# Words of the weights merged by GpSimd from the fourth item on, and the second unit's attention steps placed anew, in a one-core Trainium2 kernel

## Chip, cores, metric

The kernel runs on one core of one Trainium2 chip. The metric is the device time of one execution in microseconds (us), lower is better. "Clock" is the granted clock of TensorE as a share of full speed.

## The reference

A gated linear recurrence per head, then a two-layer block with ELU:

```python
f = 1.0 / (1.0 + np.exp(-f_logit))                      # q, k, v, f_logit: (4, 8, 768, 48)
for t in range(S):
    state = f[:, :, t, :, None] * state + np.einsum('bhd,bhe->bhde', k[:, :, t], v[:, :, t])
    y[:, :, t] = np.einsum('bhd,bhde->bhe', q[:, :, t], state)
x = y.transpose(0, 2, 1, 3).reshape(3072, 384)
h = x @ w_in                                            # w_in: (384, 2048)
g = np.where(h > 0, h, np.exp(np.minimum(h, 0)) - 1)
out = g @ w_out                                         # w_out: (2048, 384)
```

The two weights come as 64-bit floats. The kernel computes in 32 bits, so it must first turn every pair of 32-bit words into one fp32 word.

## The kernel before

The tokens are cut into 12 units of 256. While TensorE does the block for one unit (`up`: first product with the ELU behind it, `down`: second product), the attention of a later unit is worked in between, at numbered steps T. An even step does one `up`, an odd step one `down`. The weights come in 16 items, each used for the first time at its own step. An item goes through four hands: a transfer, a split on VectorE (two instructions), a lowering on ScalarE, and a merge:

```python
def split(n):
    ...
    bits = held[n] = sb.tile([128, 2 * DM], I32, tag="bits", name=f"bits{n}")     # two buffers
    nc.vector.tensor_scalar(out=bits[:], in0=hi, scalar1=3, scalar2=0x3FFFFFF8,
        op0=ALU.logical_shift_left, op1=ALU.bitwise_and)
    nc.vector.tensor_scalar(out=hi, in0=hi, scalar1=-(2**30), scalar2=None, op0=ALU.bitwise_and)

def lower(n):
    ...
    nc.scalar.activation(raw.bitcast(U16)[:, 2::4], raw.bitcast(U32)[:, 0::2], AF.Copy, scale=2.0**-29)

def merge(n):
    ...
    nc.vector.tensor_tensor(out=to.bitcast(I32), in0=bits, in1=hi, op=ALU.add)
    ...
    fetch(n + AHEAD)                                      # AHEAD = 7

def attention(u, first, then):
    ...
    at_step(then[1], lambda: advance(u))                          # TensorE: state increments
    at_step(then[2], *(lambda c=c: step(u, c) for c in range(NC)))   # VectorE: four additions
    at_step(then[3], lambda: kept.append(scores(u)), lambda: mask(u, kept[0]))
    at_step(then[4], lambda: outputs(u))
    at_step(then[5], lambda: carried(u))                          # ends with the small copies of xt
```

The schedule is manual: in the traces every engine works its instructions in the order in which this loop writes them.

```python
attention(1, (), A1)                        # second unit: A1 = (2, 4, 4, 5, 7, 9)
...
for T in range(NU * NFT):
    P = T // 2
    ...
    if T % 2 == 0 and P and order[P - 1][0] < DIRECT:
        elu(P - 1)
    for f in plan.pop(T, ()):               # attention, merges, loads of this step
        f()
    if T % 2 == 0:
        up(P)
    elif P >= LAG:
        down(P - LAG)
    for n in later.pop(T, ()):              # splits and lowerings two steps ahead of the merge
        split(n)
        lower(n)
```

The scores of the second unit use the two PSUM banks that the four additions read. And `up` of item 6 in the order (near 67 us) is the first that reads `xts[1]`, the second unit's rows. These are complete only when two copies of 48 KB, from one part of the tile to another, have landed:

```python
(nc.sync if u > 1 else nc.scalar).dma_start(
    out=x[GAP[r] : GAP[r] + PAD, 0:NKT], in_=x[frm : frm + D, NKT])
```

## Time and profile before

| | before |
|---|---|
| median, range of the first three runs | 569.17 us, 569.11 to 569.18 |
| span of the profiled run, clock | 567.4 us, 0.996 |
| TensorE waits in sum | 11.5 us, all before 44 us |
| first `up` product starts | 29.25 us |
| last down products start | 561.41 us |

A line of the waits view reads: waiting engine, tile and line, what ended the wait, then the sum, the number and the longest, in us. A line of a timeline reads: start, us, engine, line, operation, output<-input, and in brackets the idle time before it. The lines themselves stand in the prediction.

### The profile page before, as it was taken

Reading aid. Unit: us, or ns where it says so; the run is one execution under the profiler, and the core shown is the slowest. Engines: PE = TensorE matmul, PEld = TensorE weight load, DVE = VectorE, ACT = ScalarE, POOL = GpSimd, SP = SyncE. Lnnn points to the kernel's source line nnn. Section 1 sums busy time; section 2 is a strip of 40 time slices with the busy share of each in tenths; the row PEclk is TensorE's granted clock in tenths of the full one; section 3 lists DMA queues with packets and bytes.
Section 4 is the critical chain, followed back from the end, with each engine's and each line's share of the span. In section 5 each row is a group of like instructions: output and inputs, shape, how many; then the busy total and the mean of one; then the engine's idle time right before and its main releaser. Section 6 shows DMA issues by size and latency. Waiting matters only on the chain.

```text
span 567.4 us, 15202 instructions
## 1 busy us (share of the span) xinstructions
PE 550.2 (97%) x6226; PEld 501.8 (88%) x6226; DVE 395.2 (70%) x765; ACT 229.3 (40%) x417; POOL 266.3 (47%) x530
## 2 busy tenths in 40 slices
PE   6879999999999999999999999999999999999996
PEld 3457777778999999999999999999999999999995
DVE  8798485835976795885785885786786876745543
ACT  3297737334343443434333343343333343333331
POOL 6510027642374474465366357257257348325332
PEclk9998999999999999999999999999999999999999
DMA  8989780060025125215216216216206203201001
GB/s 207 259 215 297 174 223 14 2 161 29 2 50 140 58 60 143 73 45 152 79 36 155 85 37 154 84 38 154 84 20 172 84 9 72 85 2 36 29 2 35
DMA packets 37902, 53.27 MB, mean 94 GB/s; under 512 B 3680, under 2 KB 27648, under 8 KB 37824
## 3 DMA queue, kind: packets, MB, share of 16 engines
q1 hardware_dynamic: 37024, 51.62, 34.6%
q8 instruction: 51, 0.84, 0.6%
q10 hardware_dynamic: 800, 0.59, 0.5%
q14 instruction: 27, 0.22, 0.1%
HBM read 44.04 MB, written 4.72 MB: 86 GB/s over the span
## 4 chain that ended last, share of the span: by engine, by line
PE 92%; DVE 3%; DMA 2%; issue 1%; ACT 1%; POOL 1%; SPq 0%; DVEq 0%; ACTq 0%; POOLq 0%
PE psH L878 35%; PE psM L977 33%; PE psM L955 8%; PE psH L923 6%; PE psS L701 2%; PE psY L739 2%; PE psY L759 2%; PE psU_a L724 2%; PE psT L665 2%; DMA f<-f 1%; DVE f L627 1%; DMA f<-in_f_logit_dram 1%; ACT area L569 1%; DVE bits L559 0%; PE psY L804 0%
## 5 line engine op out<-in xcount | busy, mean ns | idle before, releaser
L878 PE MATMUL psH<-xt,wi 128*128 128x128 f32 (+1 forms) x960 | 177.1, 293 | 0.0
L942 POOL TENSOR_TENSOR sums<-gg 128x128 f32<-128x128 f32 x160 | 69.5, 455 | 210.8 <-DVE gg L932 202.5
L878 PEld LDWEIGHTS psH<-xt,wi 128*128 128x128 f32 x960 | 135.9, 192 | 0.8
L910 ACT ACTIVATE gg<-hh 128x512 f32<-128x512 f32 x80 | 50.5, 631 | 205.9 <-DVE hh L900 140.5
L878 PE MATMUL psH<-xt,area 128*128 128x128 f32 x640 | 110.5, 275 | 0.0
L878 PEld LDWEIGHTS psH<-xt,area 128*128 128x128 f32 x640 | 96.9, 192 | 4.1
L887 DVE TENSOR_TENSOR hh<-psH,u 128x256 f32<-128x256 f32 x80 | 33.8, 423 | 88.7 <-ACT u L885 88.7
L977 PE MATMUL psM<-area,sums 128*128 128x192 f32 x480 | 91.2, 326 | 0.0
L977 PEld LDWEIGHTS psM<-area,sums 128*128 128x128 f32 x480 | 80.1, 190 | 0.2 <-POOL sums L942 0.2
L977 PE MATMUL psM<-wo,gg 128*128 128x192 f32 x320 | 68.1, 335 | 0.0
L617 POOL TENSOR_TENSOR k<-k,f 128x256 f32<-128x256 f32 x48 | 39.4, 822 | 57.1 <-DMA area<-in_moe_w_in_dram 35.0
L627 DVE RECIPROCAL f<-f 128x256 f32<-128x256 f32 x36 | 62.8, 1747 | 1.3
L911 ACT ACTIVATE gg<-gg 128x512 f32<-128x512 f32 x96 | 60.6, 631 | 3.0
L932 DVE SCALAR_TENSOR_TENSOR gg<-gg,hh 128x512 f32<-128x512 f32 x80 | 55.7, 696 | 1.8 <-ACT gg L911 1.8
L977 PEld LDWEIGHTS psM<-wo,gg 128*128 128x128 f32 x320 | 50.2, 190 | 1.9
L900 DVE TENSOR_TENSOR hh<-psH,u43h 128x256 f32<-128x256 f32 (+1 forms) x160 | 49.8, 353 | 2.7
L923 PE MATMUL psH<-xt,wi 128*128 128x256 f32 x192 | 44.5, 381 | 1.4 <-DVE wi L577 1.2
L942 POOL TENSOR_TENSOR sums<-gg,sums 128x128 f32<-128x128 f32 x80 | 42.8, 535 | 6.3
L955 PE MATMUL psM<-wo,gg 128*128 128x384 f32 x128 | 45.4, 498 | 0.0
L885 ACT COPY u<-psH 128x128 f32<-128x128 f32 x80 | 21.0, 263 | 59.3 <-PE psH L878 59.3
L923 PEld LDWEIGHTS psH<-xt,wi 128*128 128x128 f32 x192 | 35.9, 190 | 8.6 <-issue 1.6
L900 DVE TENSOR_TENSOR u43h<-psH,hh 128x256 f32<-128x256 f32 x80 | 33.9, 423 | 13.4 <-PE psH L878 13.0
(97 smaller groups left out, 721.9 us busy)
## 6 DMA issues: line engine op xcount, KB each, us to landing
area<-in_moe_w_out_dram SPq DMA_DIRECT2D x8, 768.0 KB, 8.9
again<-in_moe_w_in_dram SPq DMA_DIRECT2D x16, 384.0 KB, 4.1
again<-in_moe_w_out_dram SPq DMA_DIRECT2D x16, 384.0 KB, 3.5
k<-in_k_dram SPq DMA_DIRECT2D x12, 384.0 KB, 4.8
q<-in_q_dram SPq DMA_DIRECT2D x12, 384.0 KB, 5.5
v<-in_v_dram SPq DMA_DIRECT2D x12, 384.0 KB, 5.9
area<-in_moe_w_in_dram SPq DMA_DIRECT2D x8, 576.0 KB, 7.2
out_dram<-o SPq DMA_DIRECT2D x38, 96.0 KB, 1.7
```

Of the source, the lines that this page charges most:

```text
L617: e.tensor_tensor(out=t[n][:, p], in0=t[n][:, p], in1=t["f"][:, p, "kq".index(n)], op=ALU.mult)
L627: nc.vector.reciprocal(f[:, p, 1], f[:, p, 0])
L878: nc.tensor.matmul(to, lhsT=lhs, rhs=rhs, start=(n == 0), stop=True, skip_group_check=True)
L887: add = lambda to, x, y: nc.vector.tensor_tensor(out=to, in0=x, in1=y, op=ALU.add)
L900: add = lambda to, x, y: nc.vector.tensor_tensor(out=to, in0=x, in1=y, op=ALU.add)
L910: nc.scalar.activation(g[:], h, AF.Relu, scale=-1.0)
L911: nc.scalar.activation(g[:], g[:], AF.Exp, scale=-1.0)
L923: nc.tensor.matmul(ph[:, i], lhsT=wi[j][:, kt, i * 128 : (i + 1) * 128], rhs=xts[m][:, kt, :], start=(kt == 0), stop=(kt == NKT - 1),)
L932: nc.vector.scalar_tensor_tensor(out=g[:], in0=g[:], scalar=-1.0, in1=phs.pop(P), op0=ALU.add, op1=ALU.max)
L942: nc.gpsimd.tensor_tensor(out=s[:, i], in0=x, in1=y, op=op)
L955: nc.tensor.matmul(pm[t][:], lhsT=g[:, i, t * 128 : (t + 1) * 128], rhs=wo[:, 2 * j + i, :], start=(j == 0 and i == 0), stop=(j == NP - 1 ...
L977: nc.tensor.matmul(pm[bank][:, half * DH : (half + 1) * DH], lhsT=x, rhs=y, start=first, stop=(j == NP - 1), skip_group_check=True,)
```

## The change

The intent is to take 13 of the 16 merges from VectorE, which was full near 40 us, to GpSimd, which was idle there, and to move the second unit's scores behind the first down product.

```diff
+    M0 = 3
...
-    A1 = (2, 4, 4, 5, 7, 9)
+    A1 = (2, 3, 4, 6, 7, 9)
...
-            nc.vector.tensor_tensor(out=to.bitcast(I32), in0=bits, in1=hi, op=ALU.add)
+            e = nc.gpsimd if n >= M0 else nc.vector
+            e.tensor_tensor(out=to.bitcast(I32), in0=bits, in1=hi, op=ALU.add)
```

## The prediction

> **What bounds the kernel now.** I read the page first: the busy shares and the chain that ended last.
>
> ```profile
> PE 550.2 (97%) x6226; PEld 501.8 (88%) x6226; DVE 395.2 (70%) x765; ACT 229.3 (40%) x417; POOL 266.3 (47%) x530
> ...
> PE 92%; DVE 3%; DMA 2%; issue 1%; ACT 1%; POOL 1%; SPq 0%; DVEq 0%; ACTq 0%; POOLq 0%
> ```
>
> TensorE holds 97% of the span and 92% of the chain. A change on VectorE and GpSimd can therefore win only what TensorE loses to waits, or to a lower clock. The view of TensorE's waits over the whole run lists nine, 12.3 us in sum (3.3 + 2.6 + 2.0 + 1.2 + 0.9 + 0.6 + 0.5 + 0.2 + 0.2), and the timeline shows all of them before 44 us. From there on TensorE has no gap. Which can the change touch? Items 0, 1 and 2 of the weights stay on VectorE, and item 3 is merged at 38.72 us, so all that lies before that moment stays. Two waits are left, both in front of the second unit's scores:
>
> ```profile
> PE psS L701 <- issue: 2.6, 1, 2.6
> ...
> PE psS L701 <- DVE state L682: 0.2, 1, 0.2
> ```
>
> "issue" says that the profile saw no releaser. The timeline of VectorE gives it: the scores (42.78 us) reuse the two banks that the four state additions read, and the third addition of four from 41.37 us, 0.46 us apart, ends just there. Why are the additions so late?
>
> ```profile
> 37.24 0.97 DVE L559 TENSOR_SCALAR bits<-area 128x768 int32<-128x768 int32 x1
> 38.24 0.57 DVE L563 TENSOR_SCALAR area<-area 128x768 int32<-128x768 int32 x1
> 38.72 0.95 DVE L577 CUSTOM_DVE_ANT_0 wo<-area,bits 128x1536 uint16<-128x1536 uint16 x1
> 39.70 0.56 DVE L559 TENSOR_SCALAR bits<-area 128x768 int32<-128x768 int32 x1
> 40.30 0.56 DVE L563 TENSOR_SCALAR area<-area 128x768 int32<-128x768 int32 x1
> 40.78 0.68 DVE L932 SCALAR_TENSOR_TENSOR gg<-gg,psH 128x512 f32<-128x512 f32 x1
> 41.37 1.77 DVE L682 TENSOR_TENSOR state<-psU_a,state 128x192 f32<-128x192 f32 x4
> ```
>
> VectorE works without a pause: a split (two instructions), the merge of item 3, a split, the activation's end, the additions. The merge at 38.72 is what the change takes away. The view by windows, cut into lengths of 3.41 us, shows that the gap costs twice (columns: length, then busy time of PE, PEld, DVE, ACT, POOL, then granted clock, DMA share, GB/s):
>
> ```profile
> 29.98:33.39 3.41, 2.16 (x11) 1.61 (x10) 2.94 (x4) 2.52 (x3) 0.73 (x1) 1.00 1.06 245
> ...
> 40.22:43.63 3.41, 0.64 (x23) 0.56 (x27) 3.00 (x9) 3.37 (x4) 0.00 (x0) 1.00 1.05 279
> 43.63:47.04 3.41, 3.41 (x59) 2.38 (x50) 3.34 (x6) 1.67 (x2) 0.00 (x0) 0.50 1.06 233
> ```
>
> After a window with 0.64 us of TensorE work the clock is 0.50 for 3.41 us: 1.7 us of work lost. A window with 2.16 us (gap 1.25 us) has no such sequel. So the place costs 2.6 + 0.2 + 1.7 = **4.5 us**, and that is the most the change can win. GpSimd is idle there:
>
> ```profile
> 72.77 0.72 POOL L617 TENSOR_TENSOR k<-k,f 128x256 f32<-128x256 f32 x1 [34.98 <-DMA area<-in_moe_w_in_dram]
> ```
>
> **What the Trainium skill says.** (1) "GPSIMD Engine Reference", 3.1, elementwise side by side: a two-input add of 2048 fp32 takes 4497 ns on GpSimd and 2293 ns on VectorE. The trace agrees in kind: GpSimd's product of 128x256 takes 0.72 us undisturbed. (2) The same page, 4.1, engine selection: an add whose tensors are all one 32-bit integer type is exact on GpSimd. No GpSimd integer add is in this trace; on VectorE the merge shows as a custom instruction over 1536 uint16, so the result should stay right. (3) "SBUF — State Buffer", who interferes with whom: a VectorE instruction in a two-port mode, or with two SBUF inputs, and a GpSimd instruction that reads SBUF exclude one another for a whole instruction. The trace agrees: the GpSimd product at 36.46 us, beside the merge on VectorE at 36.25, took 1.33 us in place of 0.72, and the split behind it, at 37.24, 0.97 in place of 0.56. (4) "TensorE: Matmul & The Clock Gate", part 1: an idle window of about 3.4 us brings the half clock. The windows above agree in length, but here 0.64 us of work did not prevent it.
>
> **The change part by part.** *Moved:* 13 of 16 merges (items 3 to 15). VectorE is rid of 13 x 0.97 = 12.6 us. GpSimd gets 13 new instructions. Estimate of one from the trace: 0.455 us for 128x128 and 0.72 for 128x256, so 0.265 us more per 128 columns, and 0.455 + 5 x 0.265 = 1.78 us for 768 columns; 13 x 1.8 = 23 us. Neither sum is on the path.
>
> *Added without being written:* splits and merges share two "bits" buffers. The split of item n + 2 may start only when the merge of item n is done. On one engine that was free; now VectorE waits for GpSimd, and GpSimd for ScalarE's lowering. With the port exclusion, both hold VectorE up.
>
> *Placement:* of the second unit, the scores go from step 5 to 6 and the advance from 4 to 3. The additions stay at 4. TensorE has nothing else in step 3, so the advance keeps its place in TensorE's order. But the first down product (step 5) now stands before the scores (step 6) and fills the hole, if item 3 is merged by then. In return the mask on VectorE comes later, behind the split of item 7 and the end of the third activation, and the outputs of step 7 need it.
>
> A ledger with the durations above (a split 1.1 us, an activation's end 0.6, a mask 1.2, a lowering 1.8, two together 3.7; up 2.6, down 2.7, scores or outputs 1.1):
> - Lowering of item 3 ends 37.96. Its merge gets the port after the first split instruction: 38.2 to 40.0. TensorE ends its up product at 40.0; down runs 40.1 to 42.8 and no longer waits for the scores.
> - VectorE's second split instruction of item 4 waits for the port until 40.0, ends 40.5; split of item 5 to 41.6; activation's end to 42.2; third addition ends 43.6, fourth 44.05. Scores begin 43.7, bulk 44.1 to 45.0: 1.1 us of gap.
> - Lowering of 4: 40.5 to 42.3, merge to 44.2; up follows, 45.0 to 47.6. Lowering of 5 to 44.1, merge 44.2 to 46.0.
> - Split of 6 waits for merge 4 and then for the port that merge 5 holds: 46.0 to 47.1. Split of 7 (its data landed at 46.1: issue at 37.8, 8.3 us to landing) to 48.2, activation's end to 48.8, mask to 50.0.
> - Outputs at 50.1, where before they began at 51.34: a new gap of 2.5 us, yet 1.2 to 1.3 us earlier, since the half clock (1.7 us) is gone while about 0.7 us of idle time came on top.
>
> Behind that TensorE sets the pace again. I checked the later meeting points in the old frame: item 13 is merged 88.1 to 89.9, then the last products of unit 2 are ready near 91.3, the transposes start at 92.6; the mixes run 5 us late near 103 us, but GpSimd stands idle for 1.4, 1.1 and 4.0 us between 106 and 118 us, so the blend at 118.4 keeps its time. Nothing changes after 125 us. Sum: 569.17 - 1.3 = **567.9 us**.
>
> **The rivals.**
> - *The hole is filled and no other opens.* For: the author moved the scores for just that. It would take the whole 4.5 us: 564.7. Against: the mask can't come before item 7 has landed (46.1), which gives 46.1 + 1.1 + 0.6 + 1.2 = 49.1 for the outputs, so even without any port conflict some 2.1 to 2.3 us are won: about 567.0.
> - *The new gap before the outputs brings the half clock in its turn.* It lies wholly between 47.05 and 50.46 in my ledger and leaves TensorE about 1 us of work there; the trace has 0.64 us as too little and 2.06 as enough. Then 1.7 us go again: about 569.6.
> - *VectorE becomes the bound through port and buffers.* If GpSimd takes the next merge before VectorE has got its split in, the additions slip by some 2 us, and a merge of over 2 us makes it likelier. Against: ScalarE's lowerings come 1.8 us apart, which leaves the port free in between. It would make about 571.
> - *Late merges collide with unit 2's scaling or the mixes,* and a wait appears near 90 us. My slack is 1.3 us; with merges of 2.5 us it is nearly gone. Up to 1 us.
>
> **Range and chances.** Centre 567.9; the good rival 567 or, with luck in the landing times, somewhat below; the bad ones 569.6 to 571. The range is 565.8 to 570.4. 2% is 11.4 us: more than twice what the place can give, and more than any loss I can construct from 13 instructions of 1.8 us next to a TensorE without gaps. Faster by over 2%: 0.01; within: 0.98; slower: 0.01.
>
> **What would show it right or wrong.** GpSimd integer adds of 128x768 at 1.6 to 2.1 us each, longer beside splits; splits on VectorE of up to 2 us where they wait for the port. In TensorE's waits, the 2.6 us before the scores gone or down to about 1, and a new wait before the first output products (line 739) of about 2.5 us. In the windows, no 0.50 after 43.6 us, perhaps one after 50.5. No TensorE wait between 60 us and the end. Wrong would be: a new wait near 90 us, a TensorE that runs through, merges far off 1.8 us, or a half clock that stays where it was.

## More of the kernel before

Between the start of the first up product and the start of TensorE's last two products lie 561.41 - 29.25 = **532.16 us**. I call this the stretch. It leaves out the start and the last stores; it is the better measure of what an order of instructions is worth, and the experiments are compared by it.

## The result

The changed kernel took 569.69 us in the median of four runs (568.47 to 570.13), the kernel before 569.14 (568.74 to 569.18). The ratio is 1.0008, with a 95% interval of 0.999 to 1.0026. A ratio here is the mean time of one kernel's fast runs over that of the other's of the same rounds, so not quite the ratio of the medians quoted. A second set of six runs gave 568.90 us against 569.00, ratio 0.9995 (0.9974 to 1.0015). The change moves the time by nothing that these runs can see. All outputs are right.

The page of the changed kernel, busy shares and the chain that ended last:

```profile
PE 551.5 (97%) x6226; PEld 502.4 (89%) x6226; DVE 389.3 (69%) x752; ACT 228.9 (40%) x417; POOL 289.7 (51%) x543
...
PE 91%; DMA 4%; POOL 1%; DVE 1%; issue 1%; ACT 1%; SPq 0%; ACTq 0%; DVEq 0%; POOLq 0%
```

VectorE is rid of 13 instructions, and GpSimd has 23.4 us more. But VectorE's busy time fell by 5.9 us only, not by the 12.6 of the merges. The time in which a VectorE instruction stands at the port (the access to SBUF that both engines share, point 3 of the prediction) counts as busy: the 32 split instructions took 24.8 us in place of 19.3, and the scaling of the state 4.4 in place of 3.2, which makes up the missing 6.7 us. TensorE's waits in front of the scores and of the first down product:

```profile
PE psS L703 <- issue: 1.6, 1, 1.6
...
PE psM L957 <- POOL wo L579: 0.5, 1, 0.5
```

Of 2.6 us, 1.6 are left, and 0.5 are new: the down product waits for the merge on GpSimd. VectorE's timeline, to be set beside that of before:

```profile
38.28 1.09 DVE L564 TENSOR_SCALAR area<-area 128x768 int32<-128x768 int32 x1
41.10 0.56 DVE L560 TENSOR_SCALAR bits<-area 128x768 int32<-128x768 int32 x1 [1.73 <-POOL wo L579]
41.69 2.08 DVE L564 TENSOR_SCALAR area<-area 128x768 int32<-128x768 int32 x1
43.69 0.67 DVE L934 SCALAR_TENSOR_TENSOR gg<-gg,psH 128x512 f32<-128x512 f32 x1
44.29 1.59 DVE L684 TENSOR_TENSOR state<-psU_a,state 128x192 f32<-128x192 f32 x4
```

and GpSimd's beside it:

```profile
38.20 0.73 POOL L619 TENSOR_TENSOR q<-q,f 128x256 f32<-128x256 f32 x1 [5.49 <-DMA f<-f]
38.88 2.18 POOL L579 TENSOR_TENSOR wo<-bits,area 128x768 int32<-128x768 int32 x1
41.41 1.95 POOL L579 TENSOR_TENSOR wi<-bits,area 128x768 int32<-128x768 int32 x1 [0.34 <-ACT area L570]
```

This is the heart of it. The merge of item 3 is gone from VectorE, yet the additions start at 44.29 us, where before they started at 41.37 (in a run whose first up product began 0.41 us earlier). The split of item 5 waited 1.73 us for the merge of item 3, and its second half then took 2.08 us in place of 0.56, since the merge of item 4 had come in between at 41.41. And the merge of item 3 itself was late: its lowering was through at 38.41 us, but GpSimd was then busy until 38.93 with the scaling of q, which had waited 5.49 us for a copy of 48 KB (`f<-f`, 5.7 us from issue to landing; 4.4 in the kernel before). The windows view (columns as in the prediction) shows the second half of the cost:

```profile
43.63:47.04 3.41, 1.64 (x45) 1.23 (x47) 3.20 (x7) 2.96 (x3) 1.25 (x1) 0.87 1.05 307
47.05:50.46 3.41, 3.41 (x41) 2.92 (x34) 3.34 (x6) 1.50 (x1) 0.59 (x1) 0.63 1.05 318
```

The half clock is still there, from about 46.2 to 49.6 us, some 2.6 us later than before. Before the outputs no gap is left in this run: TensorE came to them late enough. The net over this place can be read at the fifth up product (the one after the second unit's outputs and the second down product), counted from the first: 55.12 - 29.25 = 25.87 us before, 55.60 - 29.66 = 25.94 in the changed kernel, 53.94 - 28.09 = 25.85 in its second profile. The stretch is 561.69 - 29.66 = 532.03 us, 0.1 below that of before.

### The profile page after: what moved, and what is told of

The parts are those of the page before. It is cut to its first block, busy times and chain, and to the rows that moved or that the text cites. A ratio compares the mean times of both kernels' runs of the same rounds, so it can differ in the third digit from the quotient of the medians.

```text
span 567.3 us, 15209 instructions
## 1 busy us (share of the span) xinstructions
PE 551.5 (97%) x6226; PEld 502.4 (89%) x6226; DVE 389.3 (69%) x752; ACT 228.9 (40%) x417; POOL 289.7 (51%) x543
## 4 chain that ended last, share of the span: by engine, by line
PE 91%; DMA 4%; POOL 1%; DVE 1%; issue 1%; ACT 1%; SPq 0%; ACTq 0%; DVEq 0%; POOLq 0%
PE psH L880 35%; PE psM L979 33%; PE psM L957 7%; PE psH L925 6%; DMA area<-in_moe_w_in_dram 2%; PE psS L703 2%; PE psY L741 2%; PE psY L761 2%; PE psU_a L726 2%; PE psT L667 2%; DMA f<-f 1%; POOL k L619 1%; DMA f<-in_f_logit_dram 0%; POOL wo L579 0%; POOL q L619 0%
## 5 line engine op out<-in xcount | busy, mean ns | idle before, releaser
L902 DVE TENSOR_TENSOR hh<-psH,u43h 128x256 f32<-128x256 f32 (+1 forms) x160 | 49.6, 352 | 2.7
```

What stands on the lines that cost most here:

```text
L902: add = lambda to, x, y: nc.vector.tensor_tensor(out=to, in0=x, in1=y, op=ALU.add)
```

## The experiments

Each kernel was timed in five rounds beside the kernel before, on the same chip. The spread of a kernel's runs was 2 to 5 us, so the ratios have intervals of about plus or minus 0.2 to 0.3%. The stretch comes from one profile each; the two profiles of the changed kernel differ by 0.9 us, so smaller differences of the stretch say nothing. In the 14 profiles the first up product starts between 28.1 and 31.1 us, and this part of the spread the stretch leaves out.

| kernel | median (range), us | ratio to before, 95% | stretch, us | xt copies, issue to landing, us |
|---|---|---|---|---|
| before | 569.17 (569.11 to 569.18) | | 532.16 | 5.0 |
| changed | 569.69 (568.47 to 570.13) | 1.0008 (0.9990, 1.0026) | 532.03 | 4.4 |
| after_again | 568.90 (568.02 to 569.85) | 0.9995 (0.9974, 1.0015) | 532.93 | 5.6 |
| a1_only | 568.97 (567.95 to 570.98) | 0.9999 (0.9976, 1.0022) | 532.64 | 6.1 |
| m0_only | 570.93 (568.80 to 572.85) | 1.0025 (0.9999, 1.0051) | 536.39 | 2.3 |
| after_bits4 | 569.38 (566.38 to 571.08) | 0.9991 (0.9962, 1.0020) | 534.14 | 7.4 |
| item4_back | 569.02 (568.58 to 571.89) | 1.0006 (0.9980, 1.0032) | 532.13 | 5.6 |
| before_warm | 568.77 (567.53 to 570.47) | 0.9992 (0.9968, 1.0015) | 532.69 | 7.4 |
| down_first | 568.51 (567.80 to 571.15) | 0.9997 (0.9973, 1.0021) | 532.60 | 6.5 |
| before_late | 569.43 (566.68 to 571.61) | 1.0001 (0.9970, 1.0032) | 532.37 | 2.6 |
| warm_late | 568.30 (567.22 to 569.62) | 0.9987 (0.9963, 1.0010) | 530.84 | 2.3 |
| down_first_late | 567.34 (565.29 to 569.32) | 0.9970 (0.9943, 0.9997) | 528.38 | 2.4 |
| down_late_again | 567.20 (566.16 to 568.45) | 0.9962 (0.9941, 0.9984) | 528.50 | 2.4 |
| down_late_pool | 567.80 (565.79 to 569.49) | 0.9977 (0.9955, 0.9999) | 530.25 | 2.2 |

My theory after the result: what TensorE waits for near 40 to 50 us is VectorE's way through splits, additions and mask, and the merges on GpSimd lengthen that way by the buffers and by the port. The rivals: the placement, not the move, is what keeps the gain away; or the half clock has a cause of its own.

### The two halves of the change

The placement alone (the kernel before with the new `A1`):

> Placement alone: all merges stay on VectorE, only the second unit's advance and scores move. Theory (the way of VectorE's splits, merges and additions sets TensorE's waits): the wait of 2.6 us before the scores shrinks to under 0.5 us, since the first down product fills it, and a wait of about 2.4 us opens before the outputs (line 739), because the mask now stands behind the split of item 7 and an activation's end. Idle time stays near 3 us. If the half clock spares the new gap, 567.3 us; if it follows it, 569 us. Rival (the merges on GpSimd alone keep the change from winning): no gap before the outputs and no half clock, about 565 us.

TensorE's waits:

```profile
PE psY L739 <- DVE at L709: 2.3, 2, 2.0
...
PE psS L701 <- DVE state L682: 0.2, 1, 0.2
```

It came as the theory had it. The hole before the scores is filled, and a hole before the outputs opens in its place, since the mask now stands behind the split of item 7, the data of which had only just landed. The half clock followed the new hole (0.50 from 49.9 to 53.3 us). The placement alone gives no gain: stretch 532.64.

The move alone (the changed kernel with the old `A1`):

> Move alone: items 3 to 15 merged by GpSimd, the second unit's steps as before. Theory: the split of item 5 waits for the merge of item 3 and then loses the shared port to the merge of item 4, so the four additions end near 45.5 us as in the changed kernel, and with the scores in front of the first down product TensorE idles about 5 us instead of 2.8; the half clock stays. About 571 us or a little more, slower by 0.3 to 0.6 percent. Rival (VectorE freed of 12.6 us gets to the additions sooner): the wait before the scores is under 2 us, and the time is 568 us or less.

TensorE's longest wait in this kernel:

```profile
PE psS L703 <- issue: 6.2, 1, 6.2
```

The wait is 6.2 us, more than I had expected, and the stretch grew by 4.2 us, to 536.39. This profile is of the slowest of the six runs, and in it the copy `f<-f` took 6.9 us, so that GpSimd's scaling of q ended at 39.49 us and the merge of item 3 began 10.7 us after the first up product (9.2 in the changed kernel). Part of the 4.2 us may be due to that late copy. The rival that a freed VectorE gets to the additions sooner is refuted: they started at 44.61 us, 15.86 after the first up product, where before it was 41.37 - 29.25 = 12.12. So the move costs, and the placement of the change is what hides that cost behind the first down product. By the wall clock alone the slowdown is not clear (the interval begins at 0.9999).

### Buffer or port

Four bits buffers in place of two, in the changed kernel:

```diff
-        bits = held[n] = sb.tile([128, 2 * DM], I32, tag="bits", name=f"bits{n}")
+        bits = held[n] = sb.tile([128, 2 * DM], I32, tag="bits", name=f"bits{n}", bufs=4)
```

(the later check of the weights uses the same buffers, with the same edit).

> The changed kernel with four bits buffers in place of two, so that a split no longer waits for the merge two items before. If the buffer is what holds VectorE up: the wait of 1.7 us before the split of item 5 goes, the additions come 1.5 to 2 us earlier, the gap before the scores is under 0.5 us, and the stretch from the first up product to TensorE's last instruction falls from 532.0 by 2 us or more. If the shared port holds it up (my reading): GpSimd's merge of item 3 was queued first and keeps the port until 41.1 us in any case; splits show up as 2 us long instead of waiting, the gap stays at 1 us or more, and the stretch changes by less than 1 us.

VectorE's timeline:

```profile
38.12 1.10 DVE L560 TENSOR_SCALAR bits<-area 128x768 int32<-128x768 int32 x1
39.26 2.10 DVE L564 TENSOR_SCALAR area<-area 128x768 int32<-128x768 int32 x1
41.28 0.67 DVE L934 SCALAR_TENSOR_TENSOR gg<-gg,psH 128x512 f32<-128x512 f32 x1
```

My reading, that the port alone holds VectorE up, was wrong here, and the other was right for this place. Without the buffer's wait the first half of the split gets in ahead of the merge of item 3. The second half still stands at the port (2.10 us), but the additions start 12.69 us after the first up product instead of 14.63, and the gap before the scores is gone. Both causes are real, one after the other. The stretch, however, did not fall; it rose to 534.14, because TensorE then waited 2.1 us before the up product of 67.1 us and paid a half clock after that. The view puts this wait down to an instruction of ScalarE, a step of the third unit's gates. But by the code that product needs the xt tile, not the gates: ScalarE's own writes of xt, which were done at 59.9 us, and the two xt copies. The copies were issued from 59.3 us with 7.4 us to landing, so they came in near 67 us. That they ended the wait is worked out from this, not shown by the label. In item4_back and after_again, below, the label is wrong in the same way.

Item 4 alone back on VectorE, in the changed kernel:

```diff
-            e = nc.gpsimd if n >= M0 else nc.vector
+            e = nc.gpsimd if n >= M0 and n != 4 else nc.vector
```

> The changed kernel with item 4 alone merged by VectorE again. Port theory: the second split instruction of item 5, 2.08 us long beside the merge of item 4, is 0.56 us; the additions come about 1.3 us earlier, the gap before the scores falls from 1.6 to under 0.5 us, and the half clock after it goes. A gap of 1.5 to 2.5 us before the outputs may open in its place, as my prediction had it. Stretch from the first up product to TensorE's last instruction 530.5 to 532 us. Rival (the port does not matter): split as long as before, gap and half clock unchanged.

The second half of item 4's split, then the split of item 5, in VectorE's timeline:

```profile
38.09 2.08 DVE L564 TENSOR_SCALAR area<-area 128x768 int32<-128x768 int32 x1
40.09 0.55 DVE L560 TENSOR_SCALAR bits<-area 128x768 int32<-128x768 int32 x1
40.68 0.56 DVE L564 TENSOR_SCALAR area<-area 128x768 int32<-128x768 int32 x1
```

and GpSimd's:

```profile
36.84 0.80 POOL L619 TENSOR_TENSOR q<-q,f 128x256 f32<-128x256 f32 x1 [4.69 <-DMA f<-f]
37.89 1.86 POOL L579 TENSOR_TENSOR wo<-bits,area 128x768 int32<-128x768 int32 x1 [0.25 <-ACT area L570]
```

With no merge of item 4 beside it, the split's second half takes 0.56 us again, and the additions start 12.65 us after the first up product. The result is as the port theory had it, but this run does not prove it, since something else differs: here the copy `f<-f` landed after 4.9 us, the scaling of q was over before item 3 was lowered, and the merge of item 3 got the port between the two halves of item 4's split, the second of which took the 2.08 us. down_late_pool, below, has the same early scaling (over at 36.73 us) and the merge of item 4 on GpSimd, and its additions also start 12.65 us after the first up product. So the landing of that copy by itself can have this effect, and what sending item 4 back is worth stays open. The gap before the scores is 0.4 us, there is no half clock, and 2.3 + 0.3 us open before the outputs: almost line by line the ledger of my prediction. Even so the stretch is 532.13. Of the 0.8 us won up to the fifth up product, 0.7 went into a wait before the up product of 66.7 us, which reads the xt copies.

### Is it the gap that brings the half clock?

Four idle products in the hole of the kernel before:

```diff
+    at_step(5, lambda: warm(4, "m3"))
     attention(1, (), A1)
```

> The kernel before with four idle products of 128x512 (some 0.57 us each, 2.3 us) put in front of the second unit's scores, on a bank that is free there; their result is never read. Theory: the half clock after 43.6 us comes from the idle window alone. The clock stays at 1.00, the wait before the scores shrinks to about 0.3 us, the scores begin when they began, and the time falls by the 1.7 us of the half clock: 567.4 us. Rival (the low clock has another cause, or the idle time itself is what is paid): 0.50 still shows near 44 us and the time stays at 569.2.

TensorE's timeline, the idle products (line 1032), the scores, and the up product near 68 us:

```profile
40.66 3.60 PE L1032 MATMUL psW<-ident 128*128 128x512 f32 x8
44.18 1.16 PE L701 MATMUL psS<-q,k 64*64 64x64 f32 x64
...
67.79 2.40 PE L923 MATMUL psH<-xt,wi 128*128 128x256 f32 x10 [1.58 <-DMA xt<-xt]
```

The half clock is gone: 1.00 in every stretch from 40 to 72 us. So the cause is the idle time. (The four products took 3.6 us, not 2.3; each is two records. Counted from the first up product, the scores began 0.8 us later than in the kernel before.) But nothing was won, since TensorE waited 1.58 us for the xt copies at 67.8 us. This was the first sign of a second bound.

### The second bound

In step 5 the down product goes ahead of the scores, while VectorE's order and all merges stay as before:

```diff
+        if T == 5:
+            down(P - LAG)
         for f in plan.pop(T, ()):
             f()
         if T % 2 == 0:
             up(P)
-        elif P >= LAG:
+        elif P >= LAG and T != 5:
             down(P - LAG)
```

> The kernel before with one exchange: in step 5 the first down product goes ahead of the scores; VectorE's order and all merges stay. Theory: the down product (2.7 us) fills the hole, the mask stays ahead of the split of item 7, so no new gap before the outputs opens; the half clock goes. Waits of TensorE between 38 and 60 us under 1 us in sum; 4.0 to 4.5 us won: 564.7 to 565.2 us. Rival (the idle time moves on to the next meeting point, as in the changed kernel): a gap of 2 us or more before up of item 4 (line 923) or the outputs, 567 us or more.

TensorE's waits, the longest after the start:

```profile
PE psH L923 <- DMA xt<-xt: 2.1, 1, 2.1
```

Up to 60 us this did what it should: TensorE idles 0.3 us between 40 and 60 us, the clock is 1.00, and the fifth up product starts 22.0 us after the first instead of 25.87, so 3.9 us are won. Then 2.1 us of them go at 62.4 us, to the wait for the xt copies, and the half clock that follows (0.50 from 66 to 68 us) takes most of the rest. Neither the theory nor the rival as written foresaw it: the idle time did move on, but to a transfer. These copies were issued at 57.3 us, when the transfer engines had been full since 40 us and more, with the next items and the third unit's inputs.

The late fetches: the copies of the second unit are issued from SyncE, in its order ahead of the fetches of items 12 to 15, which are moved to step 10.

```diff
-        fetch(n + AHEAD)
+        if n + AHEAD < 12:
+            fetch(n + AHEAD)
...
-        (nc.sync if u > 1 else nc.scalar).dma_start(
+        (nc.sync if u > 0 else nc.scalar).dma_start(
...
+    for n in range(12, NFT):
+        at_step(10, lambda n=n: fetch(n))
```

> The exchange of step 5 (first down product ahead of the scores), and besides the second unit's exchange of rows (the small copies of xt) is issued ahead of the fetches of items 12 to 15, which are moved to step 10. Theory: what took back the gain of the exchange was the landing of those small copies behind a full transfer backlog (6.5 us; TensorE waited 2.1 us for them and paid the half clock after). With the fetches behind them they land in 5 us or less, the wait before the up product at about 62 us is under 0.5 us, no half clock, and from the first up product to TensorE's last instruction it takes 528 to 529 us instead of 532.2 (before) and 532.6 (exchange alone): about 565.5 us, 0.6 percent faster. Rival (the copies stand behind the second unit's own loads, not behind the fetches): still 6 us to landing, wait of 2 us, 568.5 us.

TensorE's timeline:

```profile
40.27 2.74 PE L956 MATMUL psM<-wo,gg 128*128 128x384 f32 x8
...
60.63 2.74 PE L956 MATMUL psM<-wo,gg 128*128 128x384 f32 x8
63.21 2.75 PE L924 MATMUL psH<-xt,wi 128*128 128x256 f32 x12
```

The copies land in 2.4 us, and the up product at 63.2 us follows the down product without a gap. The stretch is 528.38 us, 3.8 below that of before, as expected; the time is 0.30% lower (0.03 to 0.57), half of the 0.6% that I had expected. The rival is refuted. The edit changes the issuing engine together with the order, and no run parts the two; but in m0_only the copies were issued from ScalarE, at 64.2 us, when the transfers were nearly through, and landed in 2.3 us, which speaks for the backlog and not for the engine.

The late fetches alone:

> Control: the kernel before with the late fetches alone. There the small copies land about 1 us before they are needed, so nothing is gained: gap of 2.6 us and half clock as before, 532 us from the first up product to TensorE's last instruction, 569.2 us within the spread. Rival (late fetches help by themselves): over 1 us faster.

As the theory had it: the copies land in 2.6 us, the gap of 2.7 us and the half clock stay (the down product after the scores took 4.54 us), and the stretch is 532.37. In the kernel before, the copies landed near 65.7 us for a start at 66.75: a slack of about 1 us. **So as long as the copies were late, little more than 1 us could be won by anything that happened earlier:** in the nine profiles with the old order of the copies this up product, the seventh, never started sooner than 36.2 us after the first (down_first; 37.5 before), with the late fetches it started after 33.7 (down_first_late).

The late fetches with the idle products:

> The kernel before with both the four idle products in the hole and the late fetches, so that the row copies no longer catch what the idle products save. Theory: idle products alone gained nothing, since TensorE then waited 1.6 us for the row copies; with these out of the way the half clock's 1.7 us remain won: stretch from the first up product to TensorE's last instruction 530.5 us instead of 532.3, time about 0.3 percent below the kernel before. Rival (the half clock costs nothing by itself): stretch 532.3.

The stretch is 530.84 us, 1.5 below that of the control, where the half clock had been put at 1.7. So this is about what the half clock costs, as far as one profile each can tell. The wall clock (0.9987) is within its interval of no change.

### What the move is worth in the better order

Items 3 to 15 merged by GpSimd, in down_first_late:

> The best order so far (first down product ahead of the scores, late fetches) with items 3 to 15 merged by GpSimd. It asks what the move of the merges is worth where the order no longer hides it. Theory: splits wait for merges and for the port, the additions come 2 to 3 us later than with all merges on VectorE, gaps of 1 to 3 us open before the scores and the up products; stretch 530 to 533 us against 528.4. Rival (freeing VectorE of 12.6 us helps once the order is right): 528.4 or less.

TensorE's waits:

```profile
PE psY L761 <- ACT between L748: 1.0, 1, 1.0
...
PE psS L703 <- issue: 0.4, 1, 0.4
```

VectorE's timeline, the additions:

```profile
40.84 1.60 DVE L684 TENSOR_TENSOR state<-psU_a,state 128x192 f32<-128x192 f32 x4
```

The stretch is 530.25 us, 1.9 above the order with all merges on VectorE. The gaps are smaller than I had expected, and lie before the scores, the outputs and the carried products. The same order with all merges on VectorE, next to it on the same chip:

> The best order again, with all merges on VectorE, next to the two kernels above on one chip and for a second interval. Theory: stretch 528.4 us within 0.7, time 0.3 to 0.6 percent below the kernel before. If its first result was luck, the interval covers 1.000 well and the stretch is above 530.

528.50 us of stretch and 0.38% less time (0.16 to 0.59), which confirms the first result. This is the version to take: it beats both kernels (568.90 us for the changed one and 569.00 for the one before), with not one merge moved. Against down_late_pool the wall clock shows no clear difference; the 1.8 us are the stretch's. In this profile 1.8 us of waits came earlier, before the first up product (at 31.14 us), with 0.69 as the clock from 24 to 28 us: the start has a spread of its own that none of these kernels treats.

### The changed kernel once more

> The changed kernel once more, for its spread and a second profile. Of its first four runs two had a mean clock of 0.999 and were the slower ones (570.1 us against 568.5 and 569.3 at 0.995). Theory: the place between 40 and 67 us is decided by the moment at which the small start transfers and the second unit's row copies land, which differs from run to run, so runs are spread over some 3 us and the mean is that of the kernel before within 0.3 percent; from the first up product to TensorE's last instruction 532 us within 1.5. Rival (a real gain of 1.3 us as I predicted, hidden by few runs): mean 0.2 percent or more faster.

TensorE's waits:

```profile
PE psS L703 <- issue: 1.6, 1, 1.6
PE psY L741 <- DVE at L711: 1.5, 2, 1.3
```

Six runs from 568.02 to 569.85 us, no gain. This profile has no half clock at all. The gap before the scores is again 1.6 us, and the one before the outputs, absent from the first profile, is there with 1.5. The window from 46.9 to 50.3 us has 1.86 us of TensorE work, and no half clock followed. A wait of 0.7 us before the up product at 66.5 us came on top. So the same kernel pays in two ways, with one gap and the half clock or with two gaps and a late transfer, and both come to the time of before within 1 us.

## Why the prediction was right, and where its steps were not

The time fell within the range, 1.8 us above its centre, and within 2% as forecast. That is owed to a range that reached from a gain of 3.4 us to a loss of 1.2: the gain of 1.3 us at its centre was not seen, and the path that was to bring it failed at its first line. By its own steps:

- *What bounds the kernel; 4.5 us as the most to be won at this place.* Right for the place: down_first won 3.9 us up to the fifth up product. Wrong for the whole kernel: the xt copies had about 1 us of slack, and I had not looked at when they landed. I looked for waits that exist, not for those that an earlier TensorE would meet. This is the term that was mis-sized in the good rivals (564.7 and 567.0).
- *Cost of a merge on GpSimd, 1.78 us.* Right: 1.84 to 1.87 us where it stands alone, up to 2.37 beside VectorE. The sum of 23 us was right too (23.4).
- *The two bits buffers and the port hold VectorE up.* Right: 1.73 us of waiting and 2.08 in place of 0.56. after_bits4 takes the first away. The second is read from the timelines, where splits took 2.08 us and more beside merges and 0.56 elsewhere; item4_back agrees, but does not isolate it.
- *The ledger.* This step failed. "Its merge gets the port after the first split instruction: 38.2 to 40.0" did not happen. The step had GpSimd free when item 3 is lowered. In the profile before it was, by 0.2 us. In both profiles of the changed kernel the copy `f<-f` took 5.7 and 5.4 us in place of 4.4, and the scaling of q behind it ended 0.5 and 0.4 us after the lowering. So both halves of the split of item 4 were through first, item 4 was lowered earlier, and its merge took the port between the two halves of the split of item 5. The additions started at 44.29 us, 43.9 in the ledger's frame, where it had 42.2, and the gap lay before the scores (1.6 us) and not before the outputs. It was the third rival ("GpSimd takes the next merge before VectorE has got its split in"), which I had put at 571 us. It cost less, since the gap before the outputs shrank by as much. Where the scaling ended before the lowering (item4_back and down_late_pool, the copy landing after 4.9 us), the ledger's order came. The landing differs from run to run (4.3 to 6.9 us in the 14 profiles, with the merges moved or not), and no experiment fixed it.
- *The half clock goes.* Wrong in the first profile, right in the second. I had it as a rival at 569.6 us, for another gap.
- *VectorE is rid of 12.6 us.* It lost the instructions, but stood at the port instead, and got only 5.9 us.
- *Later meeting points.* Right from 75 us on: in both profiles of the changed kernel there is no TensorE wait between there and the end. The prediction had said from 60 us on, and the second profile has the 0.7 us at 66.5. The transposes near 93 us and the blend at 118.9 us kept their places.
- *Range.* The first three runs of before lay within 0.07 us, and I took the kernel for that steady. On other rounds it ran from 566.9 to 572.3.
- *Sums.* Two are off, without consequence: the nine waits add up to 11.5 us, not 12.3, and TensorE's up product before the gap ended at 40.18 us (42.78 less the gap of 2.60), not at 40.0.

What stays open: what the changed kernel gains with the late fetches (down_late_pool, with the merges moved but another order, comes nearest); which of the ways a given unprofiled run took, and why the start differs by up to 3 us from run to run. The windows show different work of TensorE before 30 us, but no experiment here was about it.

## What to carry to other kernels

Here the work taken from a full engine brought nothing, since the order behind it came to wait for the new owner: look for buffers that one engine reused in its own order, for a port that both use, and for what the new owner itself waits for just before. Before sizing a gain, look for the next thing that would arrive too late if everything came sooner, the small transfers behind a backlog above all; a bound with 1 us of slack does not show in any list of waits. And an exchange in the order of the busiest engine may do what the move of work was meant to do, as it did here.

## What the Trainium skill lacked or had wrong

- "SBUF — State Buffer", who interferes with whom: the exclusion was confirmed (split halves of 0.56 us took 2.08 to 2.19 beside merges of 1.85). What the section lacks is that such standing counts as busy time in the profile: VectorE lost 12.6 us of merges and its busy time fell by 5.9.
- "GPSIMD Engine Reference", 3.1: its only measured time for a two-input add is fp32 over 2048 columns. The 32-bit integer add of 128x768, with one operand at every second word, took 1.84 to 1.87 us alone. Scaled by columns, an estimate, the page's 4497 ns would give 1.69.
- "TensorE: Matmul & The Clock Gate", part 1: it speaks of an idle window and does not say how idle. Windows of 3.4 us with 0.64, 1.13 and 1.63 us of TensorE work (before, a1_only, and the changed kernel from 42.8 to 46.2 us) brought the half clock, one with 1.86 (after_again) did not, and gaps of 2.3 + 0.3 us in item4_back did not either. So the size of the gap alone does not decide; that its position does is not shown.
- "DMA: Bandwidth & Descriptors", queues, rings and completion order: engines take turns between queue rows packet by packet. The 48 KB copies on ScalarE's queue nevertheless took 4.4 to 7.4 us beside SyncE's backlog, and 2.2 to 2.6 us where little was ahead of them. I found no figure there for such a copy behind a backlog.
